# Attention and MLP on one core: products as column tiles, merges by DMA, reciprocals on VectorE, and a re-tuned order

## The chip, the core and the metric

One NeuronCore of a Trainium2 chip runs the whole program. The metric is device time in microseconds (us) of one execution, as the median of several. The engines work side by side, each through its own list in order, and wait for each other by semaphores: TensorE (PE in the profile; PEld are its weight loads), VectorE (DVE), ScalarE (ACT), GpSimd (POOL) and SyncE (SP), which here only issues DMAs.

## What is computed

```python
xn = layernorm(x)                        # x: 2048 x 448
q, k, v = split(xn @ wqkv)               # 16 heads of 28
s = softmax(q @ k.T / sqrt(28)) @ v @ wo # per head, then joined
g = silu(gelu(xn @ w1 + b1) @ w2 + b2)   # w1: 448 x 1792
out = x + s * g
```

All inputs and the output are bf16.

## The kernel before

Sixteen heads stand in G = 4 groups of four, and the 2048 queries in C = 4 chunks of 512. One (group, chunk) is a block, 16 blocks in all. In a block, one unit of work `m` is one head against one tile of 128 keys: 64 `m` per block, 1024 in all (`MTOT`). For each `m` the kernel makes a 128 x 512 score tile in a PSUM bank, takes its exponential to SBUF, and multiplies it with V.

**Three kinds of matmul.** A score (L1617 in `t_score`) has a contraction of 32, so four heads can lie in four row groups of the array: "row" mode, shape 32\*128 in the profile. The product with V (L2052 in `t_pv`) has 32 output rows per head (28 of V, one that sums the weights, padding), so four heads lie in four column groups and run side by side: "col" mode, 128\*32. All else, the projections of q and k (L1042), of v (L1390), the MLP's two (L1468, L1537) and the output projection (L2140), is a full 128\*128 product. Seven PSUM banks form `ring`, the eighth is `acc`, in which the products with V add up over a block. PSUM goes to SBUF by ScalarE (mostly the exponentials, L1671) and VectorE.

**Two ways to an exponential.** ScalarE takes two or three banks per instruction (L1671). Some key tiles go another way, four `m` (the four heads of one key tile) at a time; I call these quads, the code calls them late. VectorE makes `T`, a scaled score whose 16 bits read as bf16 are a rough exponential, by one instruction per `m` (L1901 in `p_apass`). Then `p_expq` makes two more copies with an integer constant added to the bits (L1960, 128 x 2048 at once), and the product with V takes all three, the last two with weights scaled by 0.6875 (`vs`). So a quad costs PE three passes instead of one. Where GpSimd is free, `p_expq` first adds the two shifted copies together, in four instructions (L1973), and a quad costs two passes: a merge. A quad takes three SBUF units of 128 x 2048 bf16 from a list of regions whose first content is dead (`unit_of`).

**The order** is not written by hand. A list scheduler in Python (`run`, `start_of`, `put`) plans all engines' lists before launch. Each task has a planned duration and latency; the earliest start wins, ties go by rank. `start_of` adds 0.1 us (`SWITCH`) when PE changes mode; `rate` puts a task in the other mode behind by `MP`. A table `BP`, one row per block, sets 26 parameters (how far ahead quads are taken, how many at once, when four score banks are taken in one go, and so on); `NQ` paces and caps the quads of each block. At run time only the planned order stands; when data come later than planned, the engine that waits holds up all that is behind it in its list.

**The end of a block** (`p_epi`): VectorE copies `acc` to SBUF (L2111), and the row of weight sums goes out to DRAM, comes back spread over 128 partitions (`rs`), is inverted by GpSimd with a power of -1 (L2121), goes out and comes back as a broadcast (L2126), all on SP's queue; GpSimd multiplies (L2130) and the block's part of the output projection may run (L2140). The last block is cut into three parts with an ending of its own (`p_epi4`, `p_norm4`, `p_last`).

Of the kernel before, what the change touches and what calls it, by code (L numbers as in the profile page):

```python
# [8 lines left out]
ALU = mybir.AluOpType  # L9
# [21 lines left out]
BPN = ('S4', 'QF', 'MG', 'GQ', 'GE', 'EPS', 'HP', 'JIT', 'RM', 'RG', 'WT', 'PV0', 'PVC', 'MP', 'ND4', 'LU', 'JOINT', 'LQ', 'JMAX', 'DQ', 'URG', 'SLACK', 'UR', 'QLEAD', 'QDIST', 'R3')  # L31
BP = (
# [17 lines left out]
)  # L50
NQ = (14, 15, 11, 13, 12, 16, 14, 5, 16, 15, 16, 16, 16, 16, 14, 16)
# [10 lines left out]
MG, GQ, GE = 1, 4.0, 12  # L62
GP, MP4, GL = 4.64, 1, 1.2
# [25 lines left out]
SEM, OWN = 0.07, 0.03  # L89
# [5 lines left out]
EA = 1  # L95
G3P = 0
# [15 lines left out]

class _Task:
    __slots__ = ("E", "fn", "reads", "writes", "dur", "lat", "rank", "w", "mode", "rows", "port")
# [5 lines left out]
    def __init__(self, E, fn, reads=(), writes=(), dur=0.1, lat=0.05, prio=5, w=1.0, mode="full", rows=(), port=False):  # L120
        self.E, self.fn, self.reads, self.writes = E, fn, list(reads), list(writes)
        self.dur, self.lat, self.rank, self.w = dur, lat, prio, w
        self.mode, self.rows, self.port = mode, set(rows), port
        if E == DVE:
            ov = min(OVERLAP, 0.4 * self.dur)
            self.dur, self.lat = self.dur - ov, self.lat + ov


class _Kernel:
# [55 lines left out]
    def start_of(self, t):  # L185
# [14 lines left out]
        for b in t.writes:  # L200
            mine = b.w is not None and b.w[0] is own
            if not (t.E == PE and mine):
                s = max(s, (b.tw or 0.0) + (OWN if mine else SEM))
            s = max(s, b.tr + SEM)
        return s

    def put(self, t, start=None):
# [3 lines left out]
        sem = self.evsem[t.E]  # L211
        self.evcnt[t.E] += 1
# [6 lines left out]
        self.prog[t.E].append(lambda eng, f=t.fn, s=sem: f(eng).then_inc(s, 1))  # L219
        h = (sem, self.evcnt[t.E])  # L220
# [276 lines left out]
    def alloc(self):  # L497
# [141 lines left out]
        self.s_x0b, self.s_wqk1 = self.sem("s_x0b"), self.sem("s_wqk1")  # L639
        self.s_out = [self.sem("s_out%d" % q) for q in range(14)]  # L640
# [374 lines left out]
    def t_tr(self, c, pr, h, bank, tok, prio=5):  # L1015
# [11 lines left out]
        return _Task(PE, f, K.b_xn[c % 3][2 * h:2 * h + 2] + [K.b_id], [tok], 0.225, 0.17, prio)  # L1027
# [9 lines left out]
    def t_proj(self, which, g, c, bank, tok, k, prio=5):  # L1037
        K = self
        w = (K.wq, K.wk)[which]

        def f(eng):
            return eng.matmul(bank, w[:, k, g * 128:(g + 1) * 128], K.xnT[:, k, c * 512:(c + 1) * 512],  # L1042
                              start=(k == 0), stop=(k > 0), skip_group_check=True)
        return _Task(PE, f, [K.b_wqk[which][g], K.b_pads, K.b_xnT[c][k // 2]], [tok], 0.216, 0.17, prio)
# [54 lines left out]
    def p_first(self):  # L1099
# [32 lines left out]
        def tr(pr, h):  # L1132
# [10 lines left out]
            return _Task(PE, f, K.b_xn[0][2 * h:2 * h + 2] + [K.b_id], [tok], 0.225, 0.17, 0)  # L1143
# [11 lines left out]
        def proj(which, h, k, bank, tok):  # L1155
# [8 lines left out]
            return _Task(PE, f, [K.b_wqk[which][0], K.b_pads, K.b_xnT[0][k] if h else K.b_x0h[k]], [tok], 0.218, 0.17, which)  # L1164
# [24 lines left out]
    def p_q0(self, h, bank, tok):  # L1189
# [5 lines left out]
                                               skip_group_check=True), [K.b_qsq[h], K.b_bsel], [tok], 0.11, 0.17, 0)  # L1195
# [7 lines left out]
    def p_warm(self, cond):  # L1203
# [4 lines left out]
        while cond():  # L1208
            yield _Task(PE, lambda eng: eng.matmul(bank[:, 0:256], K.ident[:, :], K.E_sb[:, 0, 0:256], start=True, stop=True),
                        [K.b_id, K.b_pads], [tok], 0.22, 0.1, 95)  # L1210
# [9 lines left out]
    def p_busy(self):  # L1220
# [3 lines left out]
        def f(eng):  # L1224
            ins = None
            for _ in range(3):
                ins = eng.matmul(K.acc[:, 0:128], K.zero[:, :], K.ident[:, :], start=False, stop=True,
                                 skip_group_check=True)
# [9 lines left out]
    def p_norm(self, g0, g1, pr=1):  # L1238
        K = self
        bank, tok = yield ("bank", lambda: True, pr)  # L1240
# [9 lines left out]
        yield _Task(PE, f, K.b_wsq[g0:g1] + [K.b_pads], [tok], 0.15 * n + 0.1, 0.1, pr, 0.15)  # L1250
# [27 lines left out]
    def p_tr(self, c, pr):  # L1278
        K = self
        bank, tok = yield ("bank", lambda: K.ln_done >= 2 * (c + 1) and K.ready(K.b_xn[c % 3], 0.5), 1.5)  # L1280
# [49 lines left out]
    def p_q(self, g, c):  # L1330
# [21 lines left out]
        yield _Task(PE, lambda eng: eng.matmul(bank2, K.bsel[:, :], qs, start=True, stop=True),  # L1352
# [27 lines left out]
    def t_v(self, ts, h0, h1, bank, tok, ks=range(KT)):  # L1380
# [3 lines left out]
        def f(eng):  # L1384
            ins = None
            for i, t in enumerate(ts):
                off = i * nh * DH
                for kt in ks:
                    ap = bass.AP(tensor=K.wv, offset=kt * WS + h0 * DH, ap=[[KT * WS, 128], [1, nh * DH]])
                    ins = eng.matmul(bank[:, off:off + nh * DH], K.xnT[:, kt, t * 128:(t + 1) * 128], ap,  # L1390
                                     start=(kt == 0), stop=(kt > 0), skip_group_check=True)
# [71 lines left out]
    def t_f1(self, c, ft, bank, tok, k, prio=None):  # L1463
# [3 lines left out]
        def f(eng):  # L1467
            return eng.matmul(bank, K.w1[:, k, ft * 128:(ft + 1) * 128], K.xnT[:, k, c * 512:(c + 1) * 512],  # L1468
                              start=(k == 0), stop=(k > 0), skip_group_check=True)
# [19 lines left out]
    def p_gelu(self):  # L1489
# [4 lines left out]
        for q, pc in enumerate(PIECES):  # L1494
# [16 lines left out]
            for f in range(f0, f0 + n):  # L1511
# [4 lines left out]
                        wr, 0.4267 * n + (0.1 if pc else 0.06) + (1.3 if q == 0 else 0), 0.05, -1)  # L1516
# [4 lines left out]
        K.tE[ACT] += 1.3  # L1521
# [5 lines left out]
    def p_f2(self, c, t):  # L1527
# [5 lines left out]
        for q in range(7):  # L1533
            def f(eng, q=q):
                ins = None
                for ft in (2 * q, 2 * q + 1):
                    ins = eng.matmul(ps, hv[:, ft, t * 128:(t + 1) * 128], K.w2[:, ft, :],  # L1537
                                     start=(ft == 0), stop=(ft == FT - 1))
# [205 lines left out]
    def unit_of(self, b, n=1):  # L1744
        K = self
        ok = [u for u in K.free_u if not (b >= 2 * C and u in (3, 4, 5, 11, 12, 13))]
        return min(ok, key=lambda u: max(max(t.tr, t.tw or 0.0) for t in K.b_U[u])) if len(ok) >= n else None
# [52 lines left out]
    def p_solo(self):  # L1800
        K = self
        while True:
# [3 lines left out]
            now = lambda: len(K.lq) > 0 and K.can(K.lq[0][0], K.now) and (K.in_gelu() or K.next_m >= MTOT or K.urgent(K.lq[0][0]))  # L1806
# [137 lines left out]
    def p_expq(self, m0, u):  # L1944
# [7 lines left out]
        for _ in range(2):  # L1952
            v = K.unit_of(b)
# [9 lines left out]
        if MG and K.next_m < 64 * (m0 // 64 + 1) - GE and K.tE[POOL] < K.now + GQ:  # L1963
            v, w = us[1:]
            for k in range(0, 4, MP4):
                if MP4 > 1:
                    W, X = K.pair(v, w)
                else:
                    W, X = K.part(v, k), K.part(w, k)
                    if len(W.shape) != len(X.shape):  # L1970
                        W, X = (x if len(x.shape) == 3 else x.rearrange("p (a b) -> p a b", b=128) for x in (W, X))
                bs = K.b_U[v][k:k + MP4], K.b_U[w][k:k + MP4]
                yield _Task(POOL, lambda eng, W=W, X=X: eng.tensor_tensor(W, W, X, ALU.add), bs[0] + bs[1], bs[0], GP * MP4 / 4, 0.05 if k + MP4 < 4 else GL, 2, port=True)  # L1973
# [270 lines left out]
```

## Time and profile before

| what | value |
|---|---|
| median of 3 runs | 425.3 us (424.57, 425.30, 426.86) |
| span of the profiled execution, first to last instruction | 425.0 us |
| busy: PE / ACT / DVE / POOL | 403.8 / 407.8 / 345.9 / 214.2 us |
| share of the span | 95 / 96 / 81 / 50 % |
| matmuls | 3705 (row 1234, col 1588, full 883 by their shapes) |
| score banks read by ScalarE's exponentials | 788 `m` |
| `m` by VectorE (L1901) | 236, so 59 quads; 16 of them merged (64 instructions of L1973) |

The profiled execution's own time is not among the runs; its span is 0.3 us under their median. "Busy" counts time in which an engine has an instruction in work; matmuls overlap in the pipe, so PE's number says less than ScalarE's. In a line, `out<-in` names what is written and read, "x" how many, and `<-` after an idle time who ended it.

### The profile page before, as it was taken

Reading aid. Unit: us, or ns where it says so; the run is one execution under the profiler, and the core shown is the slowest. Engines: PE = TensorE matmul, PEld = TensorE weight load, DVE = VectorE, ACT = ScalarE, POOL = GpSimd, SP = SyncE. Lnnn points to the kernel's source line nnn. Section 1 sums busy time; section 2 is a strip of 40 time slices with the busy share of each in tenths; the row PEclk is TensorE's granted clock in tenths of the full one; section 3 lists DMA queues with packets and bytes.
Section 4 is the critical chain, followed back from the end, with each engine's and each line's share of the span. In section 5 each row is a group of like instructions: output and inputs, shape, how many; then the busy total and the mean of one; then the engine's idle time right before and its main releaser. Section 6 shows DMA issues by size and latency. Waiting matters only on the chain.

```text
span 425.0 us, 9807 instructions
## 1 busy us (share of the span) xinstructions
PE 403.8 (95%) x3705; PEld 134.1 (32%) x3705; DVE 345.9 (81%) x588; ACT 407.8 (96%) x435; POOL 214.2 (50%) x214
## 2 busy tenths in 40 slices
PE   6999999999999999999999999999999999999985
PEld 4533222333222222222223442332222233223452
DVE  8969998579989998999975127679789968899865
ACT  6999999999999999999999999999999999999983
POOL 7590330784291405406374324677599678523720
PEclk9999999999999999999999999999999999999998
DMA  8702000010000000100230100001000010206232
GB/s 259 267 3 39 2 27 2 2 26 17 27 1 27 2 25 4 29 2 2 59 122 27 26 0 2 2 3 26 2 3 25 3 28 2 69 3 113 25 73 66
DMA packets 17721, 15.31 MB, mean 36 GB/s; under 512 B 8893, under 2 KB 14761, under 8 KB 17642
## 3 DMA queue, kind: packets, MB, share of 16 engines
q1 hardware_dynamic: 16810, 13.07, 11.3%
q0 software_dynamic: 576, 0.92, 1.7%
q8 instruction: 30, 0.49, 0.5%
q10 hardware_dynamic: 288, 0.69, 0.4%
q14 instruction: 17, 0.14, 0.1%
HBM read 12.60 MB, written 2.94 MB: 37 GB/s over the span
## 4 chain that ended last, share of the span: by engine, by line
PE 66%; DVE 14%; ACT 13%; issue 5%; POOL 1%; POOLq 0%; DVEq 0%; ACTq 0%
PE ring L1617 17%; PE acc L2052 15%; PE ring L1468 9%; PE ring L1537 9%; ACT P L1671 9%; PE ring L1042 5%; ACT h L1671 3%; DVE w L1901 3%; PE ring L2140 2%; PE ring L1438 2%; PE ring L1390 2%; DVE x_sb L1960 2%; PE ring L1058 2%; DVE h L1960 1%; DVE h L1450 1%
## 5 line engine op out<-in xcount | busy, mean ns | idle before, releaser
L1671 ACT ACTIVATE P<-ring 128x1024 bf16<-128x1024 f32 (+1 forms) x262 | 259.2, 1114 | 1.5 <-PE ring L1617 1.1
L1617 PE MATMUL ring<-qT,kT 32*128 32x512 bf16 (+2 forms) x1152 | 148.6, 359 | 6.3 <-ACT P L1671 1.7
L1671 ACT ACTIVATE h<-ring 128x1024 bf16<-128x1024 f32 (+1 forms) x82 | 86.0, 1139 | 2.0 <-PE ring L1617 1.8
L1617 PEld LDWEIGHTS ring<-qT,kT 32*128 32x128 bf16 x1152 | 40.1, 91 | 121.3 <-ACT P L1671 59.8
L2121 POOL TENSOR_TENSOR rc<-rs,mone 128x16 f32<-128x16 bf16 x15 | 46.6, 3104 | 21.5 <-DMA rs<-sums 21.4
L1537 PE MATMUL ring<-w,h 128*128 128x448 bf16 x224 | 55.0, 356 | 0.6 <-ACT xnT L1671 0.5
L1468 PE MATMUL ring<-xnT,w 128*128 128x512 bf16 x201 | 54.3, 382 | 0.8 <-DVE w L1901 0.6
L2052 PE MATMUL acc<-P,vaug 128*32 128x512 bf16 (+2 forms) x627 | 52.8, 354 | 0.0
L1901 DVE TENSOR_SCALAR x_sb<-ring 128x512 uint16<-128x512 f32 x64 | 42.8, 685 | 8.4 <-PE ring L1617 8.0
L1671 ACT ACTIVATE xnT<-ring 128x1024 bf16<-128x1024 f32 (+1 forms) x34 | 35.4, 1119 | 1.6 <-PE ring L1617 1.6
L1901 DVE TENSOR_SCALAR w<-ring 128x512 uint16<-128x512 f32 x52 | 34.4, 684 | 1.0 <-PE ring L1617 0.7
L1901 DVE TENSOR_SCALAR h<-ring 128x512 uint16<-128x512 f32 x40 | 27.0, 686 | 3.7 <-PE ring L1617 3.2
L2130 POOL TENSOR_TENSOR qT<-x_sb,E_sb 128x512 bf16<-128x512 f32 x15 | 18.1, 1209 | 22.8 <-DMA x_sb<-recs 22.6
L1345 POOL TENSOR_TENSOR qsq<-qT 128x512 bf16<-128x512 bf16 x12 | 12.7, 1071 | 32.7 <-DVE qT L1339 31.4
L1468 PEld LDWEIGHTS ring<-xnT,w 128*128 128x128 bf16 x201 | 16.5, 97 | 28.0 <-issue 9.4
L2052 PE MATMUL acc<-h,vaug 128*32 128x512 bf16 x213 | 24.7, 385 | 0.3 <-DVE w L1960 0.2
L1537 PEld LDWEIGHTS ring<-w,h 128*128 128x128 bf16 x224 | 16.1, 97 | 25.8 <-issue 15.5
L1339 DVE CAST qT<-ring 128x512 bf16<-128x512 f32 x15 | 10.3, 686 | 13.2 <-PE ring L1042 13.1
L1985 POOL TENSOR_SCALAR vs<-vaug 128x128 bf16<-128x128 bf16 x32 | 10.2, 320 | 21.0 <-PE acc L2052 10.7
L2052 PEld LDWEIGHTS acc<-P,vaug 128*32 128x32 bf16 x627 | 13.9, 95 | 16.7 <-issue 13.7
L2140 PE MATMUL ring<-wo,qT 128*128 128x448 bf16 x64 | 17.0, 386 | 2.3 <-POOL qT L2130 1.5
L1450 DVE TENSOR_SCALAR h<-ring,b1c 128x512 bf16<-128x512 f32 x23 | 17.0, 744 | 2.4 <-PE ring L1438 1.2
(232 smaller groups left out, 657.0 us busy)
## 6 DMA issues: line engine op xcount, KB each, us to landing
x_sb<-recs SPq DMA_DIRECT2D x60, 64.0 KB, 2.0
w<-in_B_w_dram SPq DMA_DIRECT2D x1, 1568.0 KB, 7.7
w<-in_B_w_dram SPq DMA_DIRECT2D x1, 1344.0 KB, 8.5
x_sb<-in_A_x_dram SPq DMA_DIRECT2D x2, 448.0 KB, 5.6
out_dram<-in_A_x_dram SPq DMA_DIRECT2D x2, 448.0 KB, 10.0
out_dram<-h POOLq DMA_DIRECT2D x4, 224.0 KB, 4.3
out_dram<-h SPq DMA_DIRECT2D x8, 112.0 KB, 1.7
h<-in_A_wqkv_dram SPq DMA_DIRECT2D x3, 168.0 KB, 5.2
```

The source lines that it names most:

```text
L1042: return eng.matmul(bank, w[:, k, g * 128:(g + 1) * 128], K.xnT[:, k, c * 512:(c + 1) * 512], start=(k == 0), stop=(k > 0), skip_group_che ...
L1450: yield _Task(DVE, lambda eng: eng.tensor_scalar(dst, bank, K.b1c[:, ft:ft + 1], None, op0=ALU.add), [tok, K.b_b1c], wr, 0.69, 0.0, 2)
L1468: return eng.matmul(bank, K.w1[:, k, ft * 128:(ft + 1) * 128], K.xnT[:, k, c * 512:(c + 1) * 512], start=(k == 0), stop=(k > 0), skip_grou ...
L1537: ins = eng.matmul(ps, hv[:, ft, t * 128:(t + 1) * 128], K.w2[:, ft, :], start=(ft == 0), stop=(ft == FT - 1))
L1617: return eng.matmul(dst, K.kT[32 * j:32 * j + 32, g, t * 128:(t + 1) * 128], K.qT[32 * j:32 * j + 32, g, c * 512 + q0:c * 512 + q0 + nq], ...
L1671: return eng.activation(reg[:, i0:i0 + n, :], src, ACTF.Exp, scale=SM_SCALE)
L1901: yield _Task(DVE, lambda eng: eng.tensor_scalar(K.part(u, k).bitcast(dt.uint16), K.like(u, bank), SM_SCALE * LOG2E * 128.0, (127.0 - EXP_ ...
L1960: yield _Task(DVE, lambda eng, W=W, T=T, i=i: eng.tensor_scalar(W.bitcast(u16), T.bitcast(u16), float(SH[i]), None, op0=ALU.add), bT, bW, ...
L2052: return eng.matmul(K.acc[32 * j:32 * j + 32, q0:q0 + nq], w, ap[:, col:col + nq] if len(ap.shape) == 2 else ap[:, col // 128:(col + nq) / ...
L2121: yield _Task(POOL, lambda eng: eng.tensor_tensor(K.rc[:, :], K.rs[:, :], K.mone[:, 0:1].to_broadcast([128, 16]), ALU.pow), [K.b_srs, K.b_ ...
L2130: yield _Task(POOL, lambda eng: eng.tensor_tensor(dst, K.rb, E, ALU.mult), [K.b_rb, tE], [K.b_onT[g][c]], 1.15, 0.05, 1, port=True)
L2140: ins = eng.matmul(ps, K.qT[:, g, c * 512 + t * 128:c * 512 + (t + 1) * 128], K.wo[:, g, :], start=(g == 0), stop=(g == G - 1))
```

## The change

1. **Column products.** A new `_mm` makes four 128 x 32 matmuls, one per column group, in place of one 128 x 128 matmul. It is used for all large products (q, k, v, both of the MLP, the output projection, the sums of q's squares, the last block's broadcast of sums, and the idle-time dummies of `p_busy`). Transposes, the first chunk's q and k and a few small ones stay full. `mode` of a task is "col" by default now.
2. **Merges by DMA.** The four GpSimd additions become one DMA issued from GpSimd's queue, SBUF to SBUF, 128 x 2048 bf16, that adds to its destination. Planned: 0.95 us to issue (`TXI`), 4.6 us to land (`TXL`). There are 26. A merge is left out where a unit lies in `vaug` (units 16 to 18).
3. **Shifts on GpSimd.** In blocks with `PS` above 0, one of a quad's two shifted copies is made by GpSimd, in two halves planned at 1.35 us each, if GpSimd is free within `PQ`.
4. **Last reciprocals.** From block 11 on (`RV`), the sums are inverted by VectorE's `reciprocal` instead of GpSimd's power.
5. **New order.** Nearly all rows of `BP` and `NQ` are others; the planned costs are corrected in places (table loads 1.3 to 1.48, `SEMW` 0.13 for a score after its reader); solo scores may wait until several banks are free (`SR`); units in `vaug` are used in their turn.

```diff
-NQ = (14, 15, 11, 13, 12, 16, 14, 5, 16, 15, 16, 16, 16, 16, 14, 16)
+NQ = (14, 6, 16, 11, 5, 16, 14, 3, 9, 15, 16, 16, 16, 13, 4, 4)
+TXI, TXL = 0.95, 4.6
+PS, PQ, SR = 0, 1.0, 1
+RV = 11
+def _mm(eng, out, w, x, start, stop):
+    ins = None
+    for q in range(0, 128, 32):
+        ins = eng.matmul(out[q:q + 32, :], w[:, q:q + 32], x, tile_position=(0, q), start=start, stop=stop, skip_group_check=True)
+    return ins
...
-            return eng.matmul(bank, K.w1[:, k, ft * 128:(ft + 1) * 128], K.xnT[:, k, c * 512:(c + 1) * 512],
-                              start=(k == 0), stop=(k > 0), skip_group_check=True)
+            return _mm(eng, bank, K.w1[:, k, ft * 128:(ft + 1) * 128], K.xnT[:, k, c * 512:(c + 1) * 512], k == 0, k > 0)
...
+            if i == PS and K.tE[POOL] < K.now + PQ and not {16, 17, 18} & {u, us[i]}:
+                for h in range(2):
+                    sl = slice(1024 * h, 1024 * h + 1024)
+                    yield _Task(POOL, lambda eng, W=W, T=T, i=i, sl=sl: eng.tensor_scalar(W[:, sl].bitcast(u16), T[:, sl].bitcast(u16), float(SH[i]), None, op0=ALU.add),
+                                bT[2 * h:2 * h + 2], bW[2 * h:2 * h + 2], 1.35, 0.05, 2, port=True)
+                    K.ln2e = 0 if i == 2 else 1
+                continue
...
-                yield _Task(POOL, lambda eng, W=W, X=X: eng.tensor_tensor(W, W, X, ALU.add), bs[0] + bs[1], bs[0], GP * MP4 / 4, 0.05 if k + MP4 < 4 else GL, 2, port=True)
+            W, X = K.unit[v], K.unit[w]
+            yield _Task(POOL, lambda eng: eng.dma_start(W, X, accum_op=ALU.add), K.b_U[v] + K.b_U[w], K.b_U[v], TXI, TXL, 2, tx=True)
...
+        if b >= RV:
+            yield _Task(DVE, lambda eng: eng.reciprocal(K.rc[:, :], K.rs[:, :]), [K.b_srs], [K.b_rc], 0.2, 0.05, 1)
+        else:
+            yield _Task(POOL, lambda eng: eng.tensor_tensor(K.rc[:, :], K.rs[:, :], K.mone[:, 0:1].to_broadcast([128, 16]), ALU.pow),
+                        [K.b_srs, K.b_pads], [K.b_rc], 3.0, 0.05, 1)
```

More of the change, by code (lines that the diff above doesn't have):

```diff
@@ L203, in start_of @@
                 s = max(s, (b.tw or 0.0) + (OWN if mine else SEM))
-            s = max(s, b.tr + SEM)
+            s = max(s, b.tr + (SEMW if t.mode == "row" and t.E == PE else SEM))
         return s
@@ L639, in alloc @@
         self.s_x0b, self.s_wqk1 = self.sem("s_x0b"), self.sem("s_wqk1")
+        self.s_tx, self.n_tx = [self.sem("s_tx%d" % q) for q in range(8)], 0
         self.s_out = [self.sem("s_out%d" % q) for q in range(14)]
@@ L1163, in f @@
                 return ins
-            return _Task(PE, f, [K.b_wqk[which][0], K.b_pads, K.b_xnT[0][k] if h else K.b_x0h[k]], [tok], 0.218, 0.17, which)
+            return _Task(PE, f, [K.b_wqk[which][0], K.b_pads, K.b_xnT[0][k] if h else K.b_x0h[k]], [tok], 0.218, 0.17, which, mode="full")
         def kproj(h):
@@ L1239, in p_norm @@
         K = self
-        bank, tok = yield ("bank", lambda: True, pr)
+        bank, tok = yield ("bank", lambda: True, pr, 1.0, "full")
         n = g1 - g0
@@ L1249, in f @@
             return ins
-        yield _Task(PE, f, K.b_wsq[g0:g1] + [K.b_pads], [tok], 0.15 * n + 0.1, 0.1, pr, 0.15)
+        yield _Task(PE, f, K.b_wsq[g0:g1] + [K.b_pads], [tok], 0.15 * n + 0.1, 0.1, pr, 0.15, mode="full")
         for b in K.b_hf[1]:
@@ L1279, in p_tr @@
         K = self
-        bank, tok = yield ("bank", lambda: K.ln_done >= 2 * (c + 1) and K.ready(K.b_xn[c % 3], 0.5), 1.5)
+        bank, tok = yield ("bank", lambda: K.ln_done >= 2 * (c + 1) and K.ready(K.b_xn[c % 3], 0.5), 1.5, 1.0, "full")
         for h in range(2):
@@ L1389, in f @@
                     ap = bass.AP(tensor=K.wv, offset=kt * WS + h0 * DH, ap=[[KT * WS, 128], [1, nh * DH]])
-                    ins = eng.matmul(bank[:, off:off + nh * DH], K.xnT[:, kt, t * 128:(t + 1) * 128], ap,
-                                     start=(kt == 0), stop=(kt > 0), skip_group_check=True)
+                    ins = _mm(eng, bank[:, off:off + nh * DH], K.xnT[:, kt, t * 128:(t + 1) * 128], ap, kt == 0, kt > 0)
             return ins
@@ L1805, in p_solo @@
                 return
-            now = lambda: len(K.lq) > 0 and K.can(K.lq[0][0], K.now) and (K.in_gelu() or K.next_m >= MTOT or K.urgent(K.lq[0][0]))
+            wide = lambda: K.tE[PE] <= K.now + 0.3 and sum(K.free_at(i) + SEM <= K.now + JOINT for i in range(len(K.banks))) >= min(SR, len(K.lq[0][2]))
+            now = lambda: len(K.lq) > 0 and K.can(K.lq[0][0], K.now) and (K.in_gelu() or K.next_m >= MTOT or K.urgent(K.lq[0][0])) and (SR < 2 or wide())
             yield ("until", lambda: now() or not K.lq)
@@ L1962, in p_expq @@
         K.ln2e = 0
-        if MG and K.next_m < 64 * (m0 // 64 + 1) - GE and K.tE[POOL] < K.now + GQ:
+        if MG and not {16, 17, 18} & set(us[1:]) and K.next_m < 64 * (m0 // 64 + 1) - GE and K.tE[POOL] < K.now + GQ:
             v, w = us[1:]
[L1965 to L1972, printed above, removed]
-                yield _Task(POOL, lambda eng, W=W, X=X: eng.tensor_tensor(W, W, X, ALU.add), bs[0] + bs[1], bs[0], GP * MP4 / 4, 0.05 if k + MP4 < 4 else GL, 2, port=True)
+            W, X = K.unit[v], K.unit[w]
+            yield _Task(POOL, lambda eng: eng.dma_start(W, X, accum_op=ALU.add), K.b_U[v] + K.b_U[w], K.b_U[v], TXI, TXL, 2, tx=True)
             K.free_u.append(w)
```

61 lines of the change are left out of this document (31 added, 30 removed), and 34 rows, old and new, of the table BP.

## The prediction

> **What bounds the kernel now.** I read the page's busy shares first, then busy time by stretches of 25 us, then the instruction groups, and last the timeline of the end. A rough 0.5% of the time, 2.1 us, is what a measurement of this kernel can tell from no change.
>
> ```profile
> PE 403.8 (95%) x3705; PEld 134.1 (32%) x3705; DVE 345.9 (81%) x588; ACT 407.8 (96%) x435; POOL 214.2 (50%) x214
> ```
>
> ScalarE is busy for 407.8 of 425.0 us, so only 17.2 us lie outside its work. The stretches (columns: length, then busy time and count of PE, PEld, DVE, ACT, POOL, then the granted clock) show where:
>
> ```profile
> 125.00:150.00 25.00, 24.09 (x202) 6.21 (x200) 24.60 (x40) 24.98 (x29) 8.79 (x5) 1.00 0.05 13
> 225.00:250.00 25.00, 25.00 (x142) 10.31 (x141) 5.88 (x10) 24.55 (x24) 10.60 (x8) 1.00 0.07 19
> 325.00:350.00 25.00, 24.81 (x215) 7.34 (x208) 20.79 (x34) 25.00 (x27) 19.20 (x16) 1.00 0.05 13
> 412.00:425.10 13.10, 8.20 (x111) 3.78 (x111) 6.56 (x16) 5.16 (x7) 0.07 (x1) 0.83 0.19 62
> ```
>
> From 26 to 400 us ScalarE is full in every stretch. VectorE is full beside it in some (24.60 of 25), has room in others, and idles in the one of the GELUs. PE is near full too: its starts in the timeline give about 18.5 us of streaming per 25 us, and some 48 changes of mode of 0.10 us. So there are two ways to be faster: take exponentials from ScalarE, or shorten start and end. The end has a loss of its own (timeline of PE):
>
> ```profile
> 410.03 0.55 PE L2140 MATMUL ring<-wo,qT 128*128 128x448 bf16 x2
> 412.12 0.55 PE L2140 MATMUL ring<-wo,qT 128*128 128x448 bf16 x2 [1.54 <-POOL qT L2130]
> ...
> 413.85 3.87 PE L2140 MATMUL ring<-wo,qT 128*128 128x448 bf16 x11
> ```
>
> PE waits 1.54 us for block 14's normalized output, and then 11 products start 0.37 us apart where the same ones take 0.19 earlier; the stretch 413.85 to 417.60 has a granted clock of 0.56. The wait costs 1.5 us and the slow clock after it 11 x 0.18 = 2.0.
>
> **Column products: 0, between -4.1 and +0.5 us.** The nearest row is the product with V, which is in that form already:
>
> ```profile
> L1468 PE MATMUL ring<-xnT,w 128*128 128x512 bf16 x201 | 54.3, 382 | 0.8 <-DVE w L1901 0.6
> L2052 PE MATMUL acc<-P,vaug 128*32 128x512 bf16 x503 | 48.4, 384 | 0.0
> L1468 PEld LDWEIGHTS ring<-xnT,w 128*128 128x128 bf16 x201 | 16.5, 97 | 28.0 <-issue 9.4
> L2052 PEld LDWEIGHTS acc<-P,vaug 128*32 128x32 bf16 x627 | 13.9, 95 | 16.7 <-issue 13.7
> ```
>
> Four of the latter start within 12 ns, and the next four 215 to 228 ns after (189 pairs of fours); full products of 512 columns follow each other at 215 to 227. For 256 and 128 columns, fours come at 109 and 56 ns, as full ones do at 110 and 56. So four column matmuls cost what one full does, with loads hidden. The 64 small products of v (112 columns) go from 49 to at most 56 ns: 0.45 us, the upper end. What is saved is the change of mode, 317 ns from a row start to a full or column start where 216 is the stream, 0.10 us each. But of 717 changes only 41 lie between full and column; all others are to or from row mode and stay. 41 x 0.10 = 4.1 us of PE time is the lower end. I take 0, since ScalarE is the one that ends last.
> On this the Trainium skill (TensorEngine Tiling (Array Packing), Restrictions) says that column tiling excludes the fast weight load; the two rows of loads, 97 and 95 ns, show no price for it. By that rule the four loads would be longer and might show; it is a rival below.
>
> **Shifts on GpSimd, more quads: -10.9, between 0 and -21.7 us.** What a quad takes off ScalarE: exponentials of two banks start 0.90 us apart (200.17, 201.07, 201.98 in the timeline), so four `m` are 1.81 us. What it asks of VectorE: 4 x 0.684 (L1901), 2 shifts (L1960) of 0.684 in the median, and 91.6 - 118 x 0.684 = 10.9 us over 59 quads, since 14 of the 118 shifts last 0.95 to 1.93 us beside GpSimd; in sum 4.29 us. With one shift on GpSimd it is 3.4. If half of today's 59 quads hand over a shift, VectorE gets 30 x 0.684 = 20.5 us, and with the additions gone from GpSimd perhaps half of the 10.9, 5: 25 us, or 6.6 quads at 3.8 each. I take 6: 6 x 1.81 = 10.9. GpSimd can bear it: it loses 16 x 4.6 (additions, 1.15 each) and 4 x 3.1 (powers), and gains 26 issues of 0.9 and 30 x 2.7, so 214 becomes about 233 of 414. PE even gains: a quad replaces two row runs (0.22 and two changes of 0.10 each) by one or two passes of 0.22. The lower end is 12 quads, if the planner also uses VectorE's idle time (66 us of the 374 between 26 and 400). The other end is 0: the caps in `NQ`, taken at no more than eight per block, fall from 125 to 110 in sum, and units or banks may be what is short.
>
> **Merges by DMA: +3.6, between -2 and +20 us.** They shorten PE by 10 more passes of 0.216, 2.2 us, worth nothing under ScalarE (all of it, -2, the lower end). Their price is a landing later than planned, since the product with V then holds up PE, the next scores, and after about 0.45 us (the half unit in hand) ScalarE. No run shows an accumulating transfer inside SBUF; the nearest:
>
> ```profile
> L2166 POOL DMA_DIRECT2D out_dram<-h x4 | 4.1, 1017 | 6.4 <-PE acc L2052 3.0 <-DVE h L2157 1.9 <-DVE qT L2102 1.3
> out_dram<-h POOLq DMA_DIRECT2D x4, 224.0 KB, 4.3
> ```
>
> 224 KB land 4.1 to 5.5 us after issue, their packets take 2.0 to 2.2 us of it. 512 KB: 4.3 if size cost nothing, 9.8 if all went by size; with 109 bytes per ns for the other 288 KB, 4.3 + 2.7 = 7.0, which I take, between the two ends by the measured packet rate. The plan has 5.55, so a lateness L of 1.45 us. PE asks for finished quads every 8 `m`, 3.6 us. A merge is asked for inside its lateness in 1.45 / 3.6 = 40% of cases, and then costs on average (L - 0.45) squared / (2 L) = 0.345 us beyond the half unit: 26 x 0.40 x 0.345 = 3.6.
> The same four issues show 1.41 us once and 0.87 to 0.92 else, and beside the long one VectorE ran L1564 and L1960. The Trainium skill (SBUF — State Buffer, SBUF: two separate sides) has a rule for it: a transfer from GpSimd's queue waits while a fast VectorE instruction keeps GpSimd from writing descriptors. By it a merge would be some 0.5 us later, the term 8.1 instead of 3.6, and the time 419.5.
>
> **Last reciprocals: -3.0, between 0 and -3.6 us.** Four powers of 3.06 us (median of L2121) go, and VectorE's reciprocal of 128 x 128 takes 0.96, so 16 columns some 0.2. For block 14 it began at 401.12, behind an addition that ended at 401.09, and ended at 404.43; four DMAs and the multiplication at 410.93 hang on it. A slow shift on VectorE (399.72 to 401.65) would have held the new one too, so it would be done at about 401.9, 2.5 us earlier, against the wait of 1.54. Then PE doesn't rest, and the slow clock has no cause: -1.5 - 2.0, of which I take 3.0 as the planner may use the earlier landing to put the projection earlier again.
>
> **The rest of the order: 0.** Corrected planned costs (gelu table 1.48, score after reader 0.13) change the order, not the work; the start is untouched, and for 26 to 400 us ScalarE has less than 4 us of idle time to win.
>
> **Sum**, against the profiled span: 425.0 + 0 - 10.9 + 3.6 - 3.0 = 414.7; with the 0.3 between span and median, 415.0.
>
> **Rivals.**
> (a) *No more quads.* Speaking for it: VectorE already has 18% of its time free, and the quads did not fill it; lower caps. Then 425.3 + 3.6 - 3.0 = 425.9, or 422 if merges are on time. Against: in 125 to 150 VectorE is the full one. Chance 0.14, half of it within 0.5%, half faster.
> (b) *Slower: PE waits for merges.* Place: the product with V behind each merge. It decides the sign from a mean stall of 13.9 / 26 = 0.53 us, that is, lateness L with (L - 0.45) squared / 7.2 = 0.53, L = 2.4, a landing at 8.0 us after issue. At 8.5 it is 26 x 0.87 = 22.6, and 425.3 - 13.9 + 22.6 = 434. For it: 9.8 us is the bound by size; a GpSimd list in which shifts and powers stand before the issue. Against: packets took only half of the 4.3. Chance 0.15.
> (c) *Twelve quads*: 415.0 - 10.8 = 404. VectorE's idle time speaks for it, units against. Chance 0.09.
> (d) *Column products don't overlap*: all four read the same moving data and fill one bank. If four took turns, the 756 converted products would cost 756 x 0.65 = 490 us: 904. The products with V fill one bank too and overlap. Chance 0.01. The weight-load rule: its price would be at most a load per product, 756 x 0.10 = 76, so 490; chance 0.01.
>
> **How the numbers follow.** Forecast 415.0 with chance 0.60; it covers 408 to 422 by its terms. Faster by over 0.5%: 0.60 + 0.07 + 0.09 = 0.76; within: 0.07; slower: 0.15 + 0.02 = 0.17. The range takes in (c) and (a) and the near part of (b): 403 to 428 leaves out most of (b), (d) and the far side of (c), about 0.19.
>
> **What would show it.** Right: L1901 with about 260 instructions instead of 236; ScalarE's exponentials reading about 764 `m`; column fours of 512 still at 215 to 228 ns; VectorE shifts without lengths over 1 us; no wait of PE for L2130 near the end, and a granted clock of 1 there. Wrong: PE waits for the accumulating DMA at L2052 of over 0.5 us, DMA landings over 8 us, ScalarE idle inside 26 to 400 us, or as many exponentials as before.

## The result: 484.0 us, slower by 13.8%

| | before | after |
|---|---|---|
| median of this measurement, us | 424.9 (424.1 to 426.9) | 484.0 (481.5 to 487.1) |
| ratio, 95% interval | 1 | 1.138 (1.132 to 1.144) |
| span of the profiled execution, us | 425.0 | 479.7 |
| mean granted clock over the span | 0.995 | 0.945 |
| gaps between matmul starts: of each what is beyond 0.2 us, where that is over 0.7 us, in sum | 5.9 us | 44.9 us |

In nearly all runs the time lies 1.75 to 2.0 us above the span of the same execution, so the profiled execution of before, with its span of 425.0 us, is one of about 426.8 us and not one at the median.

The forecast was 415.0 us, with 403 to 428 as its range. The first line of the page after says that ScalarE, full before, no longer is:

```profile
PE 420.5 (88%) x6167; PEld 147.4 (31%) x6167; DVE 344.0 (72%) x568; ACT 412.4 (86%) x425; POOL 325.8 (68%) x232
```

ScalarE is busy a little longer (412.4 us for 407.8), in a span 54.7 us longer: it idles for 67 us instead of 17. GpSimd (POOL) has gone from 214.2 to 325.8 us, where the prediction had about 233. The groups of the page after that answer to those shown of before, with the new shift on GpSimd (L1977) and ScalarE's exponentials among them (columns: busy time, mean ns of one, idle time before them and what ended it):

```profile
L1683 ACT ACTIVATE P<-ring 128x1024 bf16<-128x1024 f32 (+1 forms) x252 | 255.9, 1093 | 43.3 <-PE ring L1629 42.0
L119 PE MATMUL ring<-xnT,w 128*32 128x512 bf16 x844 | 59.1, 385 | 1.5 <-DVE x_sb L1915 1.1
L2066 PE MATMUL acc<-P,vaug 128*32 128x512 bf16 (+2 forms) x607 | 55.9, 374 | 0.0
L1977 POOL TENSOR_SCALAR w<-x_sb 128x1024 uint16<-128x1024 uint16 x10 | 29.4, 2983 | 4.7 <-DVE x_sb L1915 4.6
L119 PEld LDWEIGHTS ring<-xnT,w 128*32 128x32 bf16 x844 | 20.6, 96 | 27.2 <-issue 9.0
```

In this group of its exponentials ScalarE now waits 42.0 us for scores. The column products (L119) and their loads, 385 and 96 ns, look like the products with V before. And one half shift takes 2983 ns on average in this group; the plan has 1.35 us. Over all 60 of them it is 2.76 to 5.91 us, with a median of 2.81, and 180.9 us in sum. Who waits for them is in the trace's answer for that line:

```profile
who waited for it (us, times):
  PEld acc L2066: 24.9, 10
  PE acc L2066: 21.5, 10
```

Ten times PE stands at a product with V until GpSimd has made its copy, 21.5 us in all. The worst place, first GpSimd's timeline (start, duration) and then the stretches of 2 us (columns: length, then busy time and count of PE, PEld, DVE, ACT, POOL, then granted clock):

```profile
381.17 6.00 POOL L1977 TENSOR_SCALAR xnT<-qsq 128x1024 uint16<-128x1024 uint16 x2
387.14 6.23 POOL L1977 TENSOR_SCALAR xnT<-kT 128x1024 uint16<-128x1024 uint16 x2
```

```profile
388.00:390.00 2.00, 1.99 (x12) 0.24 (x10) 1.75 (x2) 1.02 (x1) 2.00 (x1) 0.50 0.00 0
390.00:392.00 2.00, 0.00 (x0) 0.00 (x0) 0.00 (x0) 1.02 (x1) 2.00 (x2) 0.50 0.00 0
392.00:394.00 2.00, 0.48 (x8) 0.17 (x8) 0.00 (x0) 0.00 (x0) 2.00 (x2) 0.50 0.00 0
394.00:396.00 2.00, 2.00 (x22) 0.55 (x18) 0.69 (x1) 0.85 (x1) 2.00 (x4) 0.50 0.14 27
396.00:398.00 2.00, 2.00 (x18) 0.24 (x10) 0.63 (x1) 1.48 (x2) 1.11 (x2) 0.50 1.06 195
```

GpSimd is full until 396. PE and VectorE do nothing from 390 to 392, and ScalarE does nothing from 392 to 394. The clock is at half in the wait, which ends at 393.5, and for some 6 us behind it, while PE works. So a wait is paid twice. The larger stretches show the same thing as a mean; they answer to 24.98 and 24.82 us of ScalarE before:

```profile
125.00:150.00 25.00, 20.10 (x217) 4.82 (x215) 17.68 (x28) 18.47 (x20) 24.20 (x18) 0.86 0.01 2
375.00:400.00 25.00, 17.35 (x163) 4.38 (x167) 16.33 (x23) 15.47 (x16) 23.25 (x15) 0.73 0.22 45
```

And the quads that all this was to buy are not there: 240 instructions of L1915, so 60 quads instead of 59, where about 260 were forecast. ScalarE's exponentials read 784 `m` instead of 788.

### The profile page after: what moved, and what is told of

Same layout as the page of the kernel before. It is cut to its first block, busy times and chain, and to the rows that moved or that the text cites. A ratio compares the mean times of both kernels' runs of the same rounds, so it can differ in the third digit from the quotient of the medians.

```text
span 479.7 us, 14693 instructions
## 1 busy us (share of the span) xinstructions
PE 420.5 (88%) x6167; PEld 147.4 (31%) x6167; DVE 344.0 (72%) x568; ACT 412.4 (86%) x425; POOL 325.8 (68%) x232
## 4 chain that ended last, share of the span: by engine, by line
PE 44%; POOL 20%; DVE 16%; issue 8%; DMA 7%; ACT 4%; SPq 0%; DVEq 0%; POOLq 0%; ACTq 0%
PE ring L119 20%; PE ring L1629 12%; PE acc L2066 10%; POOL x_sb L1977 4%; POOL w L1977 4%; POOL h L1977 3%; POOL kT L1977 3%; ACT P L1683 2%; DVE x_sb L1981 2%; DMA x_sb<-x_sb 2%; DVE x_sb L1915 2%; DVE h L1915 1%; ACT h L1683 1%; POOL rc L2138 1%; DVE st L968 1%
## 5 line engine op out<-in xcount | busy, mean ns | idle before, releaser
L119 PE MATMUL ring<-xnT,w 128*32 128x512 bf16 x844 | 59.1, 385 | 1.5 <-DVE x_sb L1915 1.1
L119 PE MATMUL ring<-w,h 128*32 128x448 bf16 x896 | 58.1, 368 | 1.0 <-DVE wq L1915 0.7
L1915 DVE TENSOR_SCALAR vaug<-ring 128x512 uint16<-128x512 f32 x68 | 44.7, 683 | 8.4 <-PE ring L1629 7.2
L1915 DVE TENSOR_SCALAR x_sb<-ring 128x512 uint16<-128x512 f32 x56 | 37.4, 685 | 11.6 <-PE ring L1629 11.1
L2138 POOL TENSOR_TENSOR rc<-rs,mone 128x16 f32<-128x16 bf16 x11 | 36.2, 3292 | 0.0
L1977 POOL TENSOR_SCALAR w<-x_sb 128x1024 uint16<-128x1024 uint16 x10 | 29.4, 2983 | 4.7 <-DVE x_sb L1915 4.6
L1915 DVE TENSOR_SCALAR h<-ring 128x512 uint16<-128x512 f32 x40 | 27.0, 685 | 6.9 <-PE ring L1629 6.5
L2066 PE MATMUL acc<-h,vaug 128*32 128x512 bf16 (+1 forms) x225 | 26.8, 398 | 2.7 <-DMA qsq<-wq 2.7
L119 PEld LDWEIGHTS ring<-xnT,w 128*32 128x32 bf16 x844 | 20.6, 96 | 27.2 <-issue 9.0
L1570 POOL TENSOR_TENSOR h<-w 128x448 bf16<-128x448 bf16 x12 | 17.0, 1419 | 17.6 <-DVE vaug L1915 15.6
L119 PEld LDWEIGHTS ring<-w,h 128*32 128x32 bf16 x896 | 18.2, 97 | 25.5 <-issue 15.5
L119 PE MATMUL ring<-xnT,wq 128*32 128x512 bf16 x232 | 20.5, 416 | 1.4 <-DVE h L1915 1.4
```

What stands on the lines that cost most here:

```text
L119: ins = eng.matmul(out[q:q + 32, :], w[:, q:q + 32], x, tile_position=(0, q), start=start, stop=stop, skip_group_check=True)
L1570: yield _Task(POOL, lambda eng, o=o, t=t: eng.tensor_tensor(o, sg[:, t, :], fb[:, t, :], ALU.mult), [K.b_sig[c % 2], K.b_fsb[c % 2]], [K.b ...
L1915: yield _Task(DVE, lambda eng: eng.tensor_scalar(K.part(u, k).bitcast(dt.uint16), K.like(u, bank), SM_SCALE * LOG2E * 128.0, (127.0 - EXP_ ...
L1977: yield _Task(POOL, lambda eng, W=W, T=T, i=i, sl=sl: eng.tensor_scalar(W[:, sl].bitcast(u16), T[:, sl].bitcast(u16), float(SH[i]), None, ...
L2066: return eng.matmul(K.acc[32 * j:32 * j + 32, q0:q0 + nq], w, ap[:, col:col + nq] if len(ap.shape) == 2 else ap[:, col // 128:(col + nq) / ...
L2138: yield _Task(POOL, lambda eng: eng.tensor_tensor(K.rc[:, :], K.rs[:, :], K.mone[:, 0:1].to_broadcast([128, 16]), ALU.pow), [K.b_srs, K.b_ ...
```

## The experiments

Theory A: PE waits for GpSimd's shifts, since one lasts twice its planned time. The rivals: the column products are what holds up PE (B); or the 26 transfers are (C); or the new order is bad in itself. Each group of runs has its own measurement of the kernel before, with medians from 424.9 to 426.8 us, and each ratio is taken against that.

### What the shifts cost: three ways to be rid of them

**e1_half**: the same order, GpSimd writes half of each half shift. The other 512 of each 1024 columns are left out of the computation.

```diff
-    eng.tensor_scalar(W[:, sl].bitcast(u16), T[:, sl].bitcast(u16), float(SH[i]), None, op0=ALU.add)
+    eng.tensor_scalar(W[:, sl2].bitcast(u16), T[:, sl2].bitcast(u16), float(SH[i]), None, op0=ALU.add)
+    sl2 = slice(1024 * h, 1024 * h + 512)
```

> The changed kernel with its order untouched; each of the 60 GpSimd shifts writes only the first 512 of its 1024 columns, so half of that part of the weights keeps old values (this part of the computation is left out). Theory A, GpSimd's shifts are the cause, since they last 2.8 us where 1.35 is planned: at half the columns they last about 1.4, the plan fits the chip, and the time falls from 484 to 420 to 430 us. Theory B, the column products cost it: the time stays above 470. Theory C, accumulating transfers that land late: above 465, since 26 transfers are unchanged.

Measured: 440.0 us, ratio 1.032 (1.026 to 1.037). The shifts last 1.50 us in the median, and PE's wait for them shrinks from 21.5 to 1.0 us. So by the ratios 45 us of the 59 hang on the length of this one instruction, and some 14 don't; theory A alone had 420 to 430.

**e2_ps0**: no shift on GpSimd at all, and the order planned anew.

```diff
-            if i == PS and K.tE[POOL] < K.now + PQ and not {16, 17, 18} & {u, us[i]}:
+            if False and K.tE[POOL] < K.now + PQ and not {16, 17, 18} & {u, us[i]}:
```

> The changed kernel with no shift on GpSimd at all; both shifted copies are made by VectorE, and the scheduler plans a new order for that. Theory A: 415 to 428 us, near the kernel before. Theory B and C: above 460, as column products and transfers stay.

Measured: 451.7 us, ratio 1.057 (1.052 to 1.062); slower than e1_half, though it has no such shift. Its quads are 59 (236 instructions of L1915). The planner, with this part taken out, gives another order, and its plan alone ends at 425.7 us where that of after ends at 417.3. It also has 39 merges by transfer instead of 26. The other 26 us I have not traced to a cause, so this run speaks neither for theory A nor against it.

**e3_cost**: the shift stays, and the planner is told the measured time, 2.85 instead of 1.35 us.

```diff
-   bT[2 * h:2 * h + 2], bW[2 * h:2 * h + 2], 1.35, 0.05, 2, port=True)
+   bT[2 * h:2 * h + 2], bW[2 * h:2 * h + 2], 2.85, 0.05, 2, port=True)
```

> The changed kernel with the planned time of a GpSimd half shift put right, 2.85 instead of 1.35 us; the scheduler makes a new order, with fewer shifts on GpSimd. Theory A: the loss by waiting for shifts goes, 430 to 452 us, since the table of parameters was not made for this order. Theory B or C alone: above 465.

Measured: 481.5 us, ratio 1.133 (1.125 to 1.140). A right cost did not help: the plan itself ends at 454.1 us, with 56 quads. PE's waits for L1977 are down to a single one of 3.0 us, but ScalarE now waits 25.9 us for products with V, up to 12.5 at once. So theory A's range for this run, 430 to 452, was missed too. It seems that the table `BP` fits one set of costs; that was not tested by itself. What follows from e2 and e3 is about method: a kernel that is planned anew is another kernel, not the old one less one part. All experiments below hold the order.

### Why the shift takes 2.8 us

**m1_pool** and **m2_pool** are small kernels that copy `x` to the output and leave everything else out. Between, GpSimd runs several forms of the shift on 128 x 1024 or 128 x 512, alone, and some beside 40 of VectorE's shifts; then some accumulating transfers.

> A kernel that computes nothing of the reference (it copies x to the output) and measures GpSimd by itself: shifts of 16-bit integers at 512 and 1024 columns, the same with bf16 add and bf16 multiply, additions of two bf16 tiles, a copy, accumulating transfers of 512 KB; then shifts and transfers again beside VectorE's shifts. Theory A1, the integer form is slow by itself: the integer shift of 1024 columns lasts 2.8 us alone and a bf16 one about 1.4. Theory A2, the port shared with VectorE makes it slow: alone 1.4 us, beside VectorE 2.8. Theory C: a transfer lands over 7 us beside VectorE's shifts.

Four rows of m1_pool's groups: an add with one operation beside VectorE's shifts, the same alone, the same in bf16, and two multiplications in one instruction:

```profile
L53 POOL TENSOR_SCALAR w<-t 128x1024 uint16<-128x1024 uint16 x6 | 20.8, 3462 | 0.5
L35 POOL TENSOR_SCALAR w<-t 128x1024 uint16<-128x1024 uint16 x4 | 11.1, 2765 | 11.5 <-DVE q L61 11.2
L39 POOL TENSOR_SCALAR w<-t 128x1024 bf16<-128x1024 bf16 x4 | 11.1, 2767 | 0.3
L41 POOL TENSOR_SCALAR w<-t 128x1024 bf16<-128x1024 bf16 x4 | 4.2, 1045 | 0.3
```

Alone it is 2.77 us, and as long in bf16 (L39): neither the integers nor VectorE beside it are the reason. VectorE adds 0.7 us (L53). But the product of two factors (L41) takes 1.05. So both A1 and A2 are out, and so is C: beside VectorE's shifts the transfers land 4.8 us after issue, alone after 4.6 and 4.7.

> A kernel that computes nothing of the reference (it copies x to the output). GpSimd alone, 1024 columns: a lone add, times 1 plus constant, add and add 0, add and times 1, a lone multiplication, two multiplications. Theory A3: lone forms 2.7 us, two-operation forms 1.05. Rival A4: all forms with an add 2.7. Then the two small transfers of a block's end (4 KB to DRAM, 4 KB back), twice alone, once behind three merges of 512 KB issued together, once behind one. Theory D: 1.5 to 2 us each alone, one of them 4 us or more behind three merges. Rival: under 2.5 in all cases.

The rows of m2_pool: a lone add (L50), multiply by 1 and then add (L52), add and then add 0 (L54), a lone multiplication in bf16 (L58), two of them (L60):

```profile
L54 POOL TENSOR_SCALAR w<-t 128x1024 uint16<-128x1024 uint16 x3 | 10.9, 3633 | 0.2
L50 POOL TENSOR_SCALAR w<-t 128x1024 uint16<-128x1024 uint16 x3 | 8.3, 2776 | 11.4 <-DVEq L12 11.2
L58 POOL TENSOR_SCALAR w<-t 128x1024 bf16<-128x1024 bf16 x3 | 8.3, 2776 | 0.2
L52 POOL TENSOR_SCALAR w<-t 128x1024 uint16<-128x1024 uint16 x3 | 3.1, 1047 | 0.2
L60 POOL TENSOR_SCALAR w<-t 128x1024 bf16<-128x1024 bf16 x3 | 3.1, 1047 | 0.2
```

What is slow is the form with a single operation (and add with add); with a multiplication and a second operation the same shift takes 1.05 us. Why, these runs do not show.

**e4_fast** puts that form into the kernel, same order, nothing left out:

```diff
-    eng.tensor_scalar(..., float(SH[i]), None, op0=ALU.add)
+    eng.tensor_scalar(..., 1.0, float(SH[i]), op0=ALU.mult, op1=ALU.add)
```

> The changed kernel, same order, complete; GpSimd's shift is written as times 1 and then plus the constant, two operations in one instruction, instead of plus alone. Theory A3: the lone-operation form is slow (2.77 us for a lone add of 1024 columns, integer or bf16, against 1.05 for two multiplications in the measuring kernel), so this one lasts about 1.05 to 1.4 us and the time is 430 to 440, as with half the columns. Rival A4: additions are slow in any form; then nothing changes, 484.

Measured: 439.5 us, ratio 1.033 (1.029 to 1.036). The shifts' median is 1.05 us; the largest group, in the trace's answer for that line (shortest, median and longest in ns, then first and last start in us):

```profile
L1977 POOL TENSOR_SCALAR w<-x_sb x10: 1037/1047/1369, 95.8 to 194.3; 128x1024 uint16<-128x1024 uint16 x10
```

A shift that is shorter than planned brings no more than the 1.50 us of e1_half, so the shifts are no longer what is late.

### The other 14 us: the merges' transfers

In e4_fast the longest gap of PE is 5.3 us, for VectorE (PE's waits: in total, how often, longest):

```profile
PE ring L1629 <- DVE qsq L1915: 5.3, 1, 5.3
```

The timelines there of GpSimd, of SP and of VectorE:

```profile
351.06 1.36 POOL L1987 DMA_DIRECT2D wk<-kT  x1 [4.26 <-DVE kT L1981]
352.26 1.06 POOL L1987 DMA_DIRECT2D wq<-x_sb  x1
353.47 0.86 POOL L1987 DMA_DIRECT2D h<-h  x1
```

```profile
353.56 0.50 SPq L2131 DMA_DIRECT2D sums<-E_sb  x1
357.79 0.33 SPq L2133 DMA_DIRECT2D rs<-sums  x1
363.90 0.34 SPq L2140 DMA_DIRECT2D recs<-rc  x1
```

```profile
357.29 0.69 DVE L1915 TENSOR_SCALAR qsq<-ring 128x512 uint16<-128x512 f32 x1
363.62 0.25 DVE L2136 RECIPROCAL rc<-rs 128x16 f32<-128x16 bf16 x1 [5.64 <-DMA rs<-sums]
```

Three merges go out within 2.4 us and land 5.12, 7.55 and 8.62 us after issue. The small transfers of the sums, issued at 353.56 (out) and 357.79 (back), run while these are under way: 4.2 us for the first (the next issue waits for it) and 5.8 for the second, where m2_pool has 1.6 for each alone. And VectorE's reciprocal, at the head of VectorE's list, waits 5.64 us for them; the score copies behind it, and PE behind those, wait too. In the kernel before, GpSimd's powers waited 21.4 us in all for these transfers (L2121), and the one wait of PE for a normalized output behind them was the 1.5 us for block 14. What GpSimd would have held up at this place was not run.

m2_pool has the transfers by themselves. A merge alone lands after 4.5 us, three together after 4.8, 6.7 and 8.7. A 4 KB transfer of sums holds the next issue for 1.6 us alone, 3.6 behind one merge and 5.2 behind three.

**e5_light**: as e1_half, and every merge moves 512 of its 2048 columns; three quarters of each sum are left out.

```diff
-            W, X = K.unit[v], K.unit[w]
+            W, X = K.part(v, 0), K.part(w, 0)
```

> The changed kernel with half-width shifts on GpSimd (as in the earlier run) and merges that move 512 of the 2048 columns, same order; half of the shifts and three quarters of the merges are left out of the computation. Theory D, the 512 KB transfers delay each other and the small transfers of the block's end (sums, reciprocals), for which VectorE now waits in its list: the time falls from 440 to 424 to 431 us, and the wait of VectorE for the sums disappears. Rival E, the new order is itself longer by what is left (ScalarE's idle time planned in): stays at 437 to 442.

Measured: 428.6 us, ratio 1.007 (1.003 to 1.011), 11 us under e1_half. PE's gaps over 0.7 us are 3.3 us in sum; it waits for no transfer.

**e7_three**: as e4_fast, and only the three merges above move 512 columns.

```diff
-            W, X = K.unit[v], K.unit[w]
+            W, X = (K.part(v, 0), K.part(w, 0)) if K.n_mg in (17, 18, 19) else (K.unit[v], K.unit[w])
```

> The kernel of e4_fast (shifts in two operations, same order) in which only three of the 26 merges, those issued at 351.06, 352.26 and 353.47 us there, move 512 of 2048 columns each (three quarters of these three additions are left out). Theory Q (one place: the sums of weights lie behind these three transfers, VectorE's reciprocal waits 5.64 us for them at the head of its list, PE stands still for 5.5 us and runs at a granted clock of 0.66 in the stretch after): the wait of VectorE for rs goes below 1.5 us, PE's gap near 360 goes, the clock there is 1.00, and the time falls from 439.5 to 431 to 434. Theory S (spread: each of the 26 transfers is late for PE by some tenths of a us): the time falls by 26 x 0.4 x 3 / 26, about 1 us, to 438 to 439, whatever becomes of the wait. If the wait goes and the time falls to 428.6 (what e5_light had), the other 23 merges cost nothing.

Measured: 433.2 us, ratio 1.018 (1.015 to 1.021). SP and VectorE in e7_three:

```profile
355.30 0.33 SPq L2133 DMA_DIRECT2D rs<-sums  x1
```

```profile
357.86 0.24 DVE L2136 RECIPROCAL rc<-rs 128x16 f32<-128x16 bf16 x1
```

The reciprocal waits for nothing now. One place, three of the 26 merges, is worth 6.3 us, more than half of the merges' part: theory Q. Not all, as 4.5 us stay with the other 23. Set beside e5_light's profile, e7_three's exponentials fall behind most at one more place, by 4.0 us between 404 and 407 us of e5_light. There two merges, issued at 398.59 and 400.89, land 7.4 and 9.5 us later, PE waits 1.1 us for the first (`qsq<-wq`), and the clock is at half from 408.0 to 414.8, which it is not in e5_light.

**f1_dma**: the kernel before, with its own order on PE, ScalarE, VectorE and SP, and the 11 of its 16 merges that have no unit in `vaug` made by one accumulating transfer.

```diff
-    eng.tensor_tensor(W, W, X, ALU.add)
+    eng.dma_start(W, X, accum_op=ALU.add)
```

> The kernel before, with PE's, ScalarE's, VectorE's and SP's orders untouched; only the merges (those without a unit in vaug) are made by one accumulating transfer in the place of the first of their four GpSimd additions. The prediction's term of +3.6 us: 428 to 432. Theory D, contention between transfers: near 0 here, 424 to 428, since these merges stand far apart and leave the queues free for the block's end; the loss in the changed kernel then comes from merges that stand together.

Measured: 432.3 us, ratio 1.018 (1.012 to 1.024): 7.5 us slower, above the 424 to 428 of one theory. Two of its four runs are at 430.3 and 430.4 us, two at 434.2 and 434.6, and the profile is of one of the first two: what the others lose more is not seen. In it PE waits 1.8 us for a merge (`xnT<-h`) and 2.7 us near the end for a normalized output (1.5 before). The sums of that output are late: they come back 6.0 us after issue, beside a merge and an output transfer issued at 396.73 and 397.62. So transfers meet here too, which that theory had not counted, and in an order planned for GpSimd's additions the transfer costs more than they do.

### The parts that were small

**b1_col**: the kernel before, with the column products alone (q, k, v, both of the MLP, the output projection; 719 products).

```diff
-            return eng.matmul(bank, w..., x..., start=(k == 0), stop=(k > 0), skip_group_check=True)
+            return _mm(eng, bank, w..., x..., k == 0, k > 0)
```

> The kernel before, same order, with only the column products put in (q, k, v, both MLP products, output projection). Theory A, and the prediction's term of 0 between -4.1 and +0.5: 421 to 426 us. Theory B: well above, 440 to 480.

Measured: 428.4 us, ratio 1.006 (1.003 to 1.008), so +2.4 us, from 1.3 to 3.5. Loads are hidden and fours of 512 columns start some 216 ns apart still. Between 26 and 400 us PE's and ScalarE's busy times are those of before within 0.2 us in sum. Of the 1.5 us by which the last exponential of the profiled run starts later, 0.6 are there at the first one already, as 0.8 are in f1_dma and f3_rv14, whose program starts like that of before, and 0.8 come after 396 us. What causes the 2.4 us is not settled.

**f2_rv11** and **f3_rv14**: the kernel before, same orders, with the sums inverted on VectorE for blocks 11 to 14, and for block 14 alone (`b >= 14` in place of `b >= 11`).

```diff
+        if b >= 11:
+            t.how, t.fn = "dve", lambda eng: eng.reciprocal(K.rc[:, :], K.rs[:, :])
```

> The kernel before, same orders, but the sums of blocks 11 to 14 are inverted by VectorE's reciprocal, put into VectorE's list where the plan had GpSimd's power. The prediction's term of -3.0 us: 421 to 425, no wait of PE near 410 us and no slow clock behind it. Rival: VectorE now waits in its list for the transfer of the sums, some 2 to 5 us in all, and the time is 426 to 432.

> As the run with blocks 11 to 14, but for block 14 alone, the one whose end PE waits for near 410 us. The prediction: -1.5 to -3.5 us, 422 to 425. Rival, VectorE's wait takes back what is won: 425 to 428.

f3_rv14: 423.5 us, ratio 0.9946 (0.9925 to 0.9967). The one row that cost 1.5 + 2.0 us before:

```profile
412.08 2.26 PE L2164 MATMUL ring<-wo,qT 128*128 128x448 bf16 x11
```

Eleven products take 2.26 us instead of 3.87, and nothing is waited for ahead of them. It is the only version here that beats the kernel before.

f2_rv11: 430.0 us, ratio 1.010 (1.006 to 1.014), 6.5 us behind f3_rv14, by three reciprocals of 0.24 us each. VectorE's timeline of f2_rv11 beside block 12's:

```profile
358.70 1.07 DVE L1981 TENSOR_SCALAR h<-h 128x2048 uint16<-128x2048 uint16 x1
359.69 1.64 DVE L1981 TENSOR_SCALAR x_sb<-h 128x2048 uint16<-128x2048 uint16 x1
361.25 1.51 DVE L1981 TENSOR_SCALAR kT<-xnT 128x2048 uint16<-128x2048 uint16 x1
```

Before, these three last 0.68 to 0.69 each. Here GpSimd's line is

```profile
355.83 4.94 POOL L1994 TENSOR_TENSOR x_sb<-x_sb,kT 128x512 bf16<-128x512 bf16 x4 [1.89 <-DVE kT L1981]
```

The power, which stood between these four additions and ran beside the shifts (357.26, 2.90 us), has left GpSimd's list. So the additions run in one go beside the first two shifts, and GpSimd's next product (L1579, 1.48 us for 1.03) beside the third. The Trainium skill (SBUF — State Buffer, Who interferes with whom) has a rule for it: a VectorE instruction in its fast two-port mode and one on GpSimd lock each other out. The trace agrees: some 2.2 us are lost on three shifts. PE then waits 2.12 us for a score copy, and the clock falls:

```profile
361.00:363.00 2.00, 0.39 (x3) 0.00 (x0) 2.00 (x3) 1.56 (x2) 1.92 (x2) 1.00 0.42 125
363.00:365.00 2.00, 1.50 (x6) 0.36 (x6) 1.83 (x4) 0.84 (x1) 1.92 (x3) 0.52 0.48 129
369.00:371.00 2.00, 2.00 (x9) 0.34 (x8) 0.61 (x2) 1.46 (x2) 0.00 (x0) 0.50 0.00 0
371.00:373.00 2.00, 2.00 (x16) 0.32 (x12) 1.52 (x3) 1.45 (x1) 0.00 (x0) 0.50 0.00 0
373.00:375.00 2.00, 2.00 (x27) 0.49 (x26) 0.36 (x1) 1.39 (x2) 0.00 (x0) 0.92 0.00 0
```

That this place is most of the loss is in the trace: ScalarE's exponentials start within 0.1 us of before's until 337 us, 0.8 us later by 361, and 6.2 us later from 369 on. The rival of this run had 426 to 432, but for another reason, a wait of VectorE for the sums; the four reciprocals wait for nothing.

## Why the prediction was wrong, by its steps

The runs that hold the order give the account, in us of 425.3 by the ratios: 59 from before to after, of which 45 go with the shifts' form (e4_fast), 6 with three merges (e7_three), 4.5 with the others (e5_light). 3.0 are left. The column products alone make 2.4, but in the order of before; how the 3.0 divide between them, the last reciprocals, what is left of the merges and the order itself was not separated.

- **Shifts on GpSimd, -10.9: the step that failed**, by size and by sign; measured +45 and one quad. "GpSimd can bear it" counted 30 x 2.7 us, and this 2.7 is twice the 1.35 that the planner has for a half. It was used as if a row showed it, and none does. The nearest rows of GpSimd before are L1010 (two operations, 128 x 448, 0.77 us) and L1973 (additions, 128 x 512, 1.15 us); by their columns a half would take 1.8 to 2.3 us, an estimate, and both halves 3.5 to 4.6. So they would have told that the copies come late, though not by how much. The step also weighed the shifts only as a share of GpSimd's time, and not as something that PE waits for. With the measured 2 x 2.8 = 5.6 us a quad's copy is late by 2.9 us, GpSimd's list has 30 of these, and each that PE asks for at once costs its wait, and then the slow clock. An estimate of the latter: 1 - 0.945 over 479.7 us is 26 us of lost clock in after, 1 - 0.986 over 438.5 is 6 in e4_fast. The 20 between them and the 21.5 us of waits make some 42 of the 45; part of the slow clock falls into the waits themselves, so the sum is rather too high. The other half of the step, that spare VectorE time becomes quads, was wrong too: VectorE's busy time is 344.0 us after 345.9, its share fell from 81 to 72%, and a single quad came of it. Rival (a) had that at 0.14. Why the planner took no more was not tested.
- **Merges by DMA, +3.6:** measured +11 in the order of after, for three quarters of the 26 merges' bytes, and +7.5 (4.9 to 10) in that of before with 11 merges. The landing was mis-sized the other way, 5.0 us in the median for 7.0. Beside VectorE's shifts a transfer alone lands 0.2 us later in m1_pool (4.85 for 4.64 on average), where the prediction weighed 0.5. What the sum left out were transfers that meet: the second and third of a close group land after 7.4 to 9.8 us, and the small transfers of sums behind them take 4 to 6 us instead of 1.6. Rival (b), PE waiting at the product with V, had the place and the consequence, but named the transfer; at that line PE waited 21.5 us for shifts and 7.4 for transfers.
- **Last reciprocals, -3.0:** right for block 14, -2.3 us (1.4 to 3.2 by f3_rv14's interval) by the mechanism given, the wait and the slow clock both gone. For blocks 11 to 13 nothing was costed, and there it is a loss: f2_rv11's 6.5 us, by its trace through a changed GpSimd list, and in e4_fast the 5.64 us that VectorE waits with scores behind it. The prediction did not ask what is queued behind the new wait.
- **Column products, 0, at most +0.5:** measured +2.4 (1.3 to 3.5). The loads cost nothing visible, as the rows had it; the upper end was too low, and the cause is open.
- **The rest of the order, 0:** it was taken as the planner's gain that the other terms count. The plan's own end is 417.3 us, before 415.4: by its own costs the new order brought nothing. e5_light, in which most of the shifts' and the transfers' cost is gone, still ends 3.0 us above before.

Of the signs named, PE waits at the product with V (for L1977 before all), landings over 8 us, ScalarE idle and as many exponentials as before all stood against it; VectorE's shifts still reach 3.49 us. PE's wait near the end has not gone either, it has another reason: `qsq<-wq`, a merge, 2.7 us, with a granted clock of 0.53 in the stretch behind it (460 to 465 us).

## What to carry to other kernels

A planned cost is not a row: an instruction form that no trace shows (this operation count, this engine, this size) is to be bounded by measured neighbours or measured alone, before its sum is built on it; here a second operation, one that changes no value, makes it 2.6 times faster. A wait put on an engine costs what stands behind it in that engine's list, and a small transfer comes late when large ones are under way. Undo one part with the order held; a re-planned kernel answers another question.

## What the runs showed of the hardware that was not expected

- GpSimd, 128 x 1024 of 16 bits: 2.77 us with one operation, 1.05 with multiply and add or two multiplications, 3.63 with add and add 0.
- Accumulating transfers of 512 KB inside SBUF: 4.5 to 4.7 us alone; of three in flight together the second and third land some 2 us later each (4.8, 6.7, 8.7).
- After a wait of 2.12 us in f2_rv11 the clock is at half from 363.1 until about 373, though PE works all the time from 363.5. The Trainium skill (TensorE: Matmul & The Clock Gate, What's actually happening) has at least one window of about 3.4 us for either change, idle for the slow clock and busy for the full one. This trace differs on the first: a shorter wait was enough. The way back took some 10 us, three such windows.
